# Attention and a two-layer MLP on one core: side work dealt out over the attention rounds, and one load moved from SyncE's queue to ScalarE's

## The chip, the cores and the metric

The kernel runs on 1 core of one Trainium2 chip. The metric is the device time of one execution in microseconds; lower is better. The times of the kernel before are 578.52, 578.22 and 577.88 us, median 578.22 us.

## The reference

Causal attention over 4 batches and 12 heads (sequence 448, head dimension 64), then a two-layer MLP with a PReLU on the 1792 tokens of width 768. Everything is float32.

```python
scores = scale * np.matmul(q, k.transpose(0, 1, 3, 2))
scores = np.where(mask, -1000000000.0, scores)
scores = scores - np.max(scores, axis=-1, keepdims=True)
attn = np.exp(scores)
attn = attn / (np.sum(attn, axis=-1, keepdims=True) + 1e-09)
x = np.matmul(attn, v).transpose(0, 2, 1, 3).reshape(1792, 768)
h = x @ w_in                                  # 768 x 2048
g = np.maximum(h, 0.0) + alpha * np.minimum(h, 0.0)
return g @ w_out                              # 2048 x 768
```

## The kernel before

**Attention, in rounds.** The 12 heads of a batch are taken in pairs, so there are 24 pairs of heads, numbered 0 to 23 in the order of the program. The work of a pair is spread over five rounds and the rounds overlap: round n loads pair n (`LK`, `LQ`: k and q by DMA on SP, line 473), makes the scores of pair n-1 on TensorE (`S0`, `S1`, `S2`, lines 563 and 555), masks them and takes row maxima of pair n-2 on VectorE (`MX..`, line 576), their exponentials and row sums on ScalarE (`EX..`, line 591), reciprocals on VectorE (`RC`, lines 604 and 605) and the normalisation on GpSimd (`NO..p`, line 534); transposes pair n-3 on TensorE (`PT..`, line 642) and copies the result out of PSUM to `ptf` (`C..`, ScalarE line 530 or VectorE line 532); and for pair n-4 does the products with v (`AV`, line 661, then `AH`, line 669), sums the outputs into the operands of the first GEMM (`XF`, line 693), copies out the part that is kept (`XH`, ScalarE line 530) and takes its low part (`XL`, line 723). The string `ORDER` (line 41) is this order, written out by hand; the number behind a `+` is how many rounds the step lies behind the loads, and the letter a, d or p behind it is the engine. Rounds 2 and 3 have strings of their own (`ROUNDS`, line 44), and `attention()` (line 796) changes the string for some others. Each engine takes its instructions in this order.

**V.** The first 64 rows of each causal block of 128 go through a block diagonal of V: `vd` (line 487), four buffers that GpSimd clears once (line 495) and that `load_vd(p)` (line 497, step `LW`) fills for pair p by two DMAs of 64x4x64, one for each head. `AH` of pair p multiplies by it. In the kernel before, all `LW` are issued on SP: those of pairs 0 and 1 in round 3, where the string has `LW+3 LW+2`.

**The hardware queues' semaphores.** The DMAs issued by SP and by ScalarE share eight completion semaphores (`DMAHW0` to `DMAHW7`), which the build hands out in turn over both engines; each such DMA first waits, in its engine's stream, for the DMA that had the same semaphore before it.

**Operands of the first GEMM.** It is done by a seven-product scheme of the Strassen kind. Each float32 operand is split into a high part and a low part. The sums of four weight blocks (`S1` to `S4`, `a_sum`, line 354, VectorE line 356), of pieces of x (`T1` to `T4`), their high parts (`h`, `t_hi`, on GpSimd, lines 733 and 534) and low parts (`l`, `t_lo`, line 736, VectorE line 737), the high parts of weights (`pcast` on GpSimd, line 534; `cast` on ScalarE, line 530) and their low parts (`sub`, GpSimd line 390) are needed from round 26 on. They are set into the attention rounds as side work, by tables: `EARLY` (line 26) names for each round its side steps, and `GAP`, `FRONT`, `MID`, `REAR` the same for other places. `plan_early()` (line 824) puts them in place: up to round 23, `l` and `S:` of `EARLY` go to `EG`, which stands after `LW` and before `XF` and `RC`; from round 24 on to `ED`, behind the copies `C..` of the round; those of `GAP` always to `EG`.

**After the attention** a planner (class `Plan`) orders the rest: the first GEMM (line 408), the PReLU, and the second GEMM (line 1342). Its output is the same for both kernels.

Of the kernel before, what the change touches and what calls it, by code (L numbers as in the profile page):

```python
# [23 lines left out]
QP = 128  # L24
WARM = 8
EARLY = {
# [4 lines left out]
}  # L31
GAP = {}
FRONT = {10: "LD", 16: "LD"}
MID = {26: "u u u"}
REAR = {}
# [5 lines left out]
ORDER = """  # L41
# [2 lines left out]
ROUNDS = {2: """  # L44
LK+0 LQ+0 EX10+2 EX11+2 MX00+2 EX00+2 MX01+2 EX01+2 MX20+2 EX20+2 MX21+2 EX21+2 RA+2 NO10+2p NO11+2p NO00+2p NO01+2p MX30+2 S0+1 S1+1 PT1+2 PT0+2 MX10+1 MX11+1 EX30+2 RB+2 NO20+2p NO21+2d NO30+2p
""", 3: """
LK+0 LQ+0 EX10+2 EX11+2 MX00+2 EX00+2 MX01+2 EX01+2 MX20+2 S2+2 EX20+2 MX21+2 PT2+3 EX21+2 C00+3d C20+3a C21+3d C10+3d S0+1 S1+1 SF+1 LW+3 LW+2 MX30+2 EX30+2 RC+2 NO10+2p NO11+2p NO00+2p NO01+2p NO20+2p NO21+2p NO30+2p MX10+1 MX11+1
"""}


# [143 lines left out]
def kernel(  # L194
# [10 lines left out]
    nc = tc.nc  # L205
    B, NPAIR, D, _, S = qt.shape
# [4 lines left out]
    LQ = S - NQ * QP  # L211
# [249 lines left out]
    T, vs, p3, masks, qd, vd = {}, [], [], [], [], []  # L461

    def half(j):
        return slice(j * D, (j + 1) * D)
# [32 lines left out]
    def load_vd(p):  # L497

        b, hp = pairs[p]
        for j in range(2):  # L500
            x = v[b, hp, :LQ, j]
            stride = x.ap[0][0]
            x = bass.AP(tensor=x.tensor, offset=x.offset, ap=[list(x.ap[0]), [(QP - CP) * stride + 2 * D, NQ + 1], list(x.ap[-1])])
            nc.sync.dma_start(out=vd[p % 4][half(j), :, j], in_=x)

    def load_v(b):
        for hs, n in ((hs, n) for hs in ((slice(0, NK), slice(NK, NPAIR)) if b == 0 else (slice(0, NPAIR),)) for n in range(NQ)):
# [242 lines left out]
    def t_four():  # L750
# [4 lines left out]
        "LV": load_v_next, "RC": row_rec, "RA": lambda p: row_rec(p, slice(0, 4)),  # L755
        "RB": lambda p: row_rec(p, slice(4, 2 * NQ + 1)), "AV": av, "AH": av_halves,
        "PTH": transpose_halves, "LW": load_vd, "BB": lambda p: None, "XH": x_hi, "XF": x_sums, "XL": x_lo,
        "ST": lambda p: flush(stores), "XN": lambda p: None, "LT": lambda p: None,
    }
# [25 lines left out]
    def order_of(text):  # L785
        order = []
        for w in text.split():
            name, lag = w.split("+")
            if name in choice:
                eng = {"a": nc.scalar, "d": nc.vector, "p": nc.gpsimd}[lag[-1]]  # L790
                order.append((int(lag[:-1]), name, lambda p, fn=choice[name], eng=eng: fn(p, eng)))
            else:
                order.append((int(lag), name, steps[name]))
        return order

    def attention(hooks):
        order, first = order_of(ORDER), {n: order_of(x) for n, x in ROUNDS.items()}

        for n in (5, 6, 7, 11, 12, 13, 20, 21, 22, 23):
            text = ORDER.replace("C00+3a", "C00+3d") if n in (5, 6, 11, 20, 22) else ORDER  # L800
            if n in (6, 7, 12, 13, 21, 23):
                text = text.replace("C30+4a ", "").replace("MX20+2 ", "MX20+2 C30+4d ")
            first[n] = order_of(text)
        first[1], first[4] = order_of(ORDER.replace("LW+1 ", "")), order_of(ORDER.replace("C00+3a", "C00+3d").replace("LW+1", "LW+2 LW+1"))

        text = ORDER.replace("C10+3a ", "").replace("EH+4 ", "EH+4 C10+3a ").replace("PT2+3 ", "PT2+3 PTH+3 ")
        first[26] = order_of(text.replace("C21+3d ", "C21+3d C30+3d "))
        first[27] = order_of(ORDER.replace("PTH+4 ", "").replace("C30+4a ", ""))
        last = max(lag for lag, *_ in order)
        for n in range(len(pairs) + last):  # L810
            for lag, name, fn in first.get(n, order):
                if 0 <= n - lag < len(pairs):
                    fn(n - lag)
                    for hook in hooks.get((n - lag, name), ()):
                        hook()
# [8 lines left out]
    def plan_early():  # L824
        for table, to in ((EARLY, plan), (GAP, gap), (FRONT, front), (MID, mid), (REAR, behind_it)):
            for n, todo in table.items():
# [50 lines left out]
    def ready_bank():  # L877

        b = ring.popleft()
        nc.tensor.matmul(b[:, :S], wi[0, "A11"][:, 0, :P], x1h[:, 0, 0], start=True, stop=True, skip_group_check=True)  # L880
        return b
# [66 lines left out]
    with tc.manual_schedule():  # L948
# [15 lines left out]
        for t in masks:  # L964
# [5 lines left out]
            out=mk, in_=mk, pattern=[[-1, QP]], compare_op=ALU.is_ge, fill=NEG, base=0,  # L970
# [22 lines left out]
        after(last, "LT", scores_over)  # L993
        after(last, "AH", attention_over)
        attention(hooks)
        t13, t24 = (tf[:, 2 * i : 2 * i + 2].rearrange("p a k n -> p (a k n)") for i in range(2))
        rooms["t"], rooms["v"] = Slots([]), Slots([])
# [6 lines left out]
        v_, z, y, x = ring.popleft(), ready_bank(), ring.popleft(), ring.popleft()  # L1004
# [544 lines left out]
```

## Time and profile before

| what | value |
|---|---|
| median of the three runs | 578.22 us |
| profiled execution, its own time | 578.1 us |
| span of that execution in the profile | 576.3 us |
| TensorE matmul busy | 566.0 us (98%) |
| VectorE busy | 471.2 us (82%) |
| ScalarE busy | 385.2 us (67%) |
| GpSimd busy | 290.5 us (50%) |

The span is what the profile sees between the first and the last instruction; the device time of the same execution is 1.8 us longer. In the profile PE is TensorE's matmuls, PEld its weight loads, DVE VectorE, ACT ScalarE, POOL GpSimd and SP SyncE, which only issues DMAs; "ACTq", "SPq" and "POOLq" are the streams that issue them. L669 is line 669 of the kernel. In a timeline a row is a run of like instructions: start, time from the first start to the last end, engine, line, tiles (written <- read), size, count; in brackets the idle time of the engine just before, and what ended it.

### The profile page before, as it was taken

What the parts mean: (1) busy time and instruction counts of PE and PEld (TensorE: products, weight loads), DVE (VectorE), ACT (ScalarE), POOL (GpSimd) and SP (SyncE); (2) the same over time, 40 slices, a digit from 0 to 9 for tenths busy, and PEclk for the clock granted to TensorE, in tenths of its full rate; (3) what the DMA queues carried; (4) which work ended last, traced back from release to release, by engine and by line L of the source; (5) the groups of instructions that cost most, each with busy time, mean ns of one, the idle gap of its engine ahead of it and who ended that gap; (6) DMA issues with size and microseconds to landing.
All of it is one profiled execution on the core that took longest, in us unless ns stands there. A gap on an engine that the chain in (4) does not pass through costs nothing.

```text
span 576.3 us, 11537 instructions
## 1 busy us (share of the span) xinstructions
PE 566.0 (98%) x3921; PEld 502.0 (87%) x3921; DVE 471.2 (82%) x988; ACT 385.2 (67%) x905; POOL 290.5 (50%) x338
## 2 busy tenths in 40 slices
PE   7999999999999999999999999999989999999997
PEld 4677767777788999999999999999989999999997
DVE  5798899999769887678877687798997899797763
ACT  5899987989778565665657556696755666665431
POOL 7766678897732543444445431446145543357420
PEclk9999999999999999999999999999999999999999
DMA  7755845644246575747777656692353424412532
GB/s 177 205 131 147 218 124 153 179 116 125 82 148 209 201 250 208 259 176 231 260 226 233 199 201 221 200 341 99 101 156 110 117 66 130 129 46 83 184 110 109
DMA packets 94074, 95.92 MB, mean 166 GB/s; under 512 B 24096, under 2 KB 83136, under 8 KB 94016
## 3 DMA queue, kind: packets, MB, share of 16 engines
q1 hardware_dynamic: 93168, 93.65, 53.2%
q0 software_dynamic: 528, 1.08, 0.6%
q8 instruction: 31, 0.51, 0.4%
q10 hardware_dynamic: 320, 0.46, 0.3%
q14 instruction: 27, 0.22, 0.1%
HBM read 66.85 MB, written 28.31 MB: 165 GB/s over the span
## 4 chain that ended last, share of the span: by engine, by line
PE 79%; DVE 14%; ACT 4%; issue 2%; DMA 1%; POOL 1%; ACTq 0%; DVEq 0%; POOLq 0%
PE bank L408 36%; PE bank L1342 32%; DVE bank L576 4%; PE bank L563 3%; ACT p L591 3%; PE bank L642 3%; PE bank L661 2%; DVE x1l L737 1%; DVE ptf L532 1%; PE bank L669 1%; PE bank L633 1%; DVE tf L693 1%; DMA kr<-in_k_dram 1%; DVE sm L604 1%; DVE nm L576 1%
## 5 line engine op out<-in xcount | busy, mean ns | idle before, releaser
L534 POOL TENSOR_SCALAR p<-p,rs 128x320 f32<-128x320 f32 (+3 forms) x165 | 83.4, 525 | 38.4 <-DVE rs L605 22.9
L1342 PE MATMUL bank<-x1h,x1l 128*128 128x384 f32 x540 | 98.7, 335 | 1.0 <-DVE x1h L1279 0.9
L1342 PEld LDWEIGHTS bank<-x1h,x1l 128*128 128x128 f32 x540 | 94.3, 188 | 1.6 <-DVE x1h L1279 1.2
L591 ACT ACTIVATE p<-bank,nm 128x192 f32<-128x192 f32 (+3 forms) x168 | 81.6, 510 | 16.4 <-DVE nm L576 15.9
L576 DVE CUSTOM_DVE_ANT_0 bank<-bank,mask 128x192 f32<-128x192 f32 (+3 forms) x168 | 70.4, 487 | 6.2 <-PE bank L563 5.8
L432 ACT ACTIVATE tf<-bank 128x448 f32<-128x448 f32 x64 | 34.5, 544 | 40.9 <-PE bank L408 30.9
L563 PE MATMUL bank<-kr,qr 64*128 64x320 f32 (+2 forms) x288 | 52.7, 451 | 1.0 <-DMA kr<-in_k_dram 0.5
L436 DVE SCALAR_TENSOR_TENSOR tf<-tf,om,bank 128x448 f32<-128x448 f32 x64 | 41.8, 676 | 6.8 <-ACT tf L432 6.5
L408 PE MATMUL bank<-x1h,wir 128*128 128x448 f32 x192 | 44.7, 368 | 0.0
L1342 PE MATMUL bank<-x1h,gset 128*128 128x384 f32 x216 | 40.4, 338 | 0.9 <-DVE acc L1355 0.9
L563 PEld LDWEIGHTS bank<-kr,qr 64*128 64x128 f32 x288 | 29.1, 186 | 11.7 <-ACT p L591 3.2
L1342 PEld LDWEIGHTS bank<-x1h,gset 128*128 128x128 f32 x216 | 37.9, 188 | 1.2 <-ACT acc L1476 1.2
L642 PE MATMUL bank<-ident,p 128*128 128x128 f32 x288 | 37.5, 278 | 1.5 <-POOL p L534 1.4
L408 PEld LDWEIGHTS bank<-x1h,wir 128*128 128x128 f32 x192 | 35.9, 188 | 3.4
L331 POOL TENSOR_TENSOR dec<-dec,tf 128x768 int32<-128x768 int32 x11 | 22.1, 2005 | 30.0 <-ACT tf L432 15.8
L591 ACT ACTIVATION_READ_ACCUMULATOR p<-bank,nm 128x1 f32 x168 | 36.9, 219 | 0.0
L530 ACT ACTIVATE ptf<-bank 128x384 f32<-128x384 f32 (+2 forms) x81 | 35.1, 499 | 2.6 <-PE bank L642 1.6
L661 PE MATMUL bank<-ptf,v 128*64 128x384 f32 (+2 forms) x288 | 36.1, 380 | 0.0
L1320 POOL TENSOR_TENSOR x1l<-acc,x1l 128x512 fp32r<-128x512 f32 x12 | 16.4, 1364 | 39.1 <-ACT x1l L1316 30.1
L422 DVE TENSOR_TENSOR bank<-bank,tf 128x448 f32<-128x448 f32 x30 | 18.9, 631 | 20.8 <-PE bank L408 18.2
L642 PEld LDWEIGHTS bank<-ident,p 128*128 128x128 f32 x288 | 31.1, 140 | 4.5 <-POOL p L534 2.9
L408 PE MATMUL bank<-x1h,wie 128*128 128x448 f32 x144 | 33.4, 367 | 0.0
(196 smaller groups left out, 1399.9 us busy)
## 6 DMA issues: line engine op xcount, KB each, us to landing
gd<-tf SPq DMA_DIRECT2D x64, 224.0 KB, 2.0
tf<-gd SPq DMA_DIRECT2D x28, 256.0 KB, 4.5
acc<-gd SPq DMA_DIRECT2D x28, 256.0 KB, 4.4
dec<-in_moe_w_in_dram SPq DMA_DIRECT2D x9, 768.0 KB, 5.2
tf<-in_moe_w_in_dram SPq DMA_DIRECT2D x7, 768.0 KB, 4.6
dec<-in_moe_w_out_dram SPq DMA_DIRECT2D x7, 768.0 KB, 4.8
tf<-in_moe_w_out_dram SPq DMA_DIRECT2D x7, 768.0 KB, 4.3
dec<-wd SPq DMA_DIRECT2D x13, 384.0 KB, 4.7
```

What stands on the lines that cost most here:

```text
L331: nc.gpsimd.tensor_tensor(out=y, in0=y, in1=low, op=ALU.add)
L408: nc.tensor.matmul(ps, w[:, u, k * P : (k + 1) * P], x[:, k], start=(st in ("P1", "P5") and i == 0), stop=(i == len(mms) - 1), skip_group_ ...
L432: nc.scalar.activation(t, bank_of(g, b, role), AF.Relu, scale=-1.0)
L436: stt(out=t, in0=t, scalar=om[:, f : f + 1], in1=bank_of(g, b, role), op0=ALU.mult, op1=ALU.add)
L530: eng.activation(out, x, AF.Copy, scale=side)
L534: eng.tensor_scalar(out=out, in0=x, scalar1=side, scalar2=1.0, op0=ALU.mult, op1=ALU.mult)
L563: nc.tensor.matmul(ps[:, o : o + lim], T["q", p][half(j), i * QP : (i + 1) * QP], T["k", p][half(j), :lim], start=(o == 0), stop=(n > 0 or ...
L576: nc.vector.tensor_tensor_reduce(out=t, in0=t, in1=mask_of(i), scale=-SCALE, scalar=MOST_F32, op0=ALU.add, op1=ALU.min, accum_out=nm,)
L591: nc.scalar.activation(T["p", p, i][:, j, : t.shape[1]], t, AF.Exp, scale=-1.0, bias=T.pop(("nm", p, i, j)), accum_out=T["sm", p][:, z : z ...
L642: nc.tensor.transpose(ps[:, j - js[0], c], t[:, j, c * QP : (c + 1) * QP], T["ident"])
L661: nc.tensor.matmul(out[half(j), c * QP + LQ :], vs[b % 2][:, hp, c, j], x[:, : (NQ - c) * QP], start=(c == 0), stop=False, skip_group_chec ...
L1342: nc.tensor.matmul(ps, x, w, start=(st in ("P1", "P5")[: 1 if Q else 2] and i == 0), stop=(i == len(mms) - 1), skip_group_check=True,)
```

## The change

It has three parts.

1. **`vd` of pair 0 goes through ScalarE's queue.** `load_vd` issues on `nc.scalar` for pair 0 and on `nc.sync` for the others. The step moves from round 3 (`LW+3` is gone from its string) to round 1 (`LQ+0 LW+1`), where the work of ScalarE is the opening of the program.
2. **The side work is dealt out again.** S2 goes from round 17 to 18, S3 from 18 to 24, S4 from 21 to 25. The low parts of x's sums, two in each of rounds 20, 23 and 24 and none in 21, 25 and 26 before, are one in each of rounds 18 to 26. One `h` goes from round 13 to round 23, so that there is one in each of rounds 11, 12 and 14 to 23. The counts are the same: four sums, twelve low parts, twelve high parts.
3. **One PSUM copy changes engine.** In round 11 the copy `C30` (line 530 on ScalarE) is done on VectorE (line 532), after the first maximum of 448 columns.

```diff
-    4: "LD", 5: "A:0", ... 11: "A:1 h", 12: "l I:1 C:1 h", 13: "D:1 h",
-    14: "G:1:0 +:1:0 h 4", 15: "G:1:1 +:1:1 4 h", 16: "l l 4 h", 17: "S:S1 S:S2 h pcast:A11", 18: "S:S3 l h sub:A11 pcast:S1",
-    19: "l sub:S1 h pcast:S2", 20: "l l sub:S2 h A:2", 21: "S:S4 h C:2", 22: "l h I:2", 23: "l l", 24: "l l",
-    25: "cast:A12 cast:S3 sub:A12 sub:S3", 26: "cast:S4 cast:A22 sub:S4 sub:A22 LD",
+    4: "LD", 5: "A:0", ... 11: "A:1 h", 12: "l I:1 C:1 h", 13: "D:1",
+    14: "G:1:0 +:1:0 h 4", 15: "G:1:1 +:1:1 4 h", 16: "l l 4 h", 17: "S:S1 h pcast:A11", 18: "S:S2 l h sub:A11 pcast:S1",
+    19: "l sub:S1 h pcast:S2", 20: "l sub:S2 h A:2", 21: "l h C:2", 22: "l h I:2", 23: "l h", 24: "S:S3 l",
+    25: "S:S4 cast:A12 cast:S3 sub:A12 sub:S3", 26: "cast:S4 cast:A22 sub:S4 sub:A22 LD",
-GAP = {}
+GAP = {25: "l", 26: "l"}
...
# ROUNDS[3]
-... S0+1 S1+1 SF+1 LW+3 LW+2 MX30+2 ...
+... S0+1 S1+1 SF+1 LW+2 MX30+2 ...
...
# load_vd
-            nc.sync.dma_start(out=vd[p % 4][half(j), :, j], in_=x)
+            (nc.sync if p else nc.scalar).dma_start(out=vd[p % 4][half(j), :, j], in_=x)
...
# attention()
-            if n in (6, 7, 12, 13, 21, 23):
+            if n in (6, 7, 11, 12, 13, 21, 23):
                 text = text.replace("C30+4a ", "").replace("MX20+2 ", "MX20+2 C30+4d ")
...
-        first[1], ... = order_of(ORDER.replace("LW+1 ", "")), ...
+        first[1], ... = order_of(ORDER.replace("LW+1 ", "").replace("LQ+0", "LQ+0 LW+1")), ...
```

Three places show the order of instructions.

ScalarE's stream at the start of the program, before: `mask` is the causal mask, `p` the exponentials of pair 0; in square brackets the semaphores that an instruction waits for.

```order
L973 ACT_TABLE_LOAD
L973 ACTIVATE mask_147<-tf 128x128 [waits Pool_49]
L976 ACTIVATE mask_148<-tf 64x64 x2
L591 ACTIVATE p_1_206,sm_207<-bank_62,nm_1_0_194 128x320 [waits DVE_49]
L591 ACTIVATE p_1_206,sm_207<-bank_63,nm_1_1_196 128x320 [waits DVE_49]
```

The same place in the changed kernel:

```order
L973 ACT_TABLE_LOAD
L973 ACTIVATE mask_147<-tf 128x128 [waits Pool_49]
L976 ACTIVATE mask_148<-tf 64x64 x2
L504 DMA vd_171<-in_v_dram 64x4x64 [waits DMAHW5_49,Pool_49]
L504 DMA vd_171<-in_v_dram 64x4x64 [waits DMAHW7_49]
L591 ACTIVATE p_1_208,sm_209<-bank_62,nm_1_0_196 128x320 [waits DVE_49]
L591 ACTIVATE p_1_208,sm_209<-bank_63,nm_1_1_198 128x320 [waits DVE_49]
```

The two DMAs now stand ahead of every exponential. Each waits for the DMA that had its semaphore before: `DMAHW5` is that of SP's first load of v below, `DMAHW7` that of SP's first half of k of pair 3.

SP's stream at the same time, in the changed kernel; before, the two rows of `vd_171` stood between `qd_102` and `vd_173`, with waits for `DMAHW5` and `DMAHW6`.

```order
L512 DMA v_167<-in_v_dram 80x3x128 [waits DMAHW5_49]
L512 DMA v_167<-in_v_dram 48x3x128 [waits DMAHW6_49]
L473 DMA kr_257<-in_k_dram 64x448 [waits DMAHW7_49,PE_49]
L473 DMA kr_257<-in_k_dram 64x448 [waits DMAHW0_49]
L473 DMA qr_260<-in_q_dram 64x384 [waits DMAHW1_49,DMASW0_49]
L473 DMA qr_260<-in_q_dram 64x384 [waits DMAHW2_49]
L477 DMA qd_102<-in_q_dram 64x3x64 [waits DMAHW3_49,DVE_49]
L477 DMA qd_102<-in_q_dram 64x3x64 [waits DMAHW4_49]
L504 DMA vd_173<-in_v_dram 64x4x64 [waits DMAHW6_49,Pool_49]
L504 DMA vd_173<-in_v_dram 64x4x64 [waits DMAHW0_49]
```

The order of SP's other DMAs is as before, and so are the semaphores of all that stand ahead of `vd_173`.

VectorE's stream in round 25, before, from the last maximum of the round to the start of round 26's side work: `x1l` is a low part, `tf` a sum of x, `sm` and `rs` the row sums and their reciprocals, `dec` a piece of weights.

```order
L576 ISA nm_3_0_2428 128x1
L693 TENSOR_TENSOR tf<-bank_65,tf 128x448
L604 TENSOR_TENSOR sm_2402<-sm_2402,least 128x7
L605 RECIPROCAL rs_2448<-sm_2402 128x7
L612 TENSOR_SCALAR p_1_2401<-p_1_2401,rs_2448 128x320 x2
L532 COPY ptf_2470<-bank_62 128x3x128
L319 TENSOR_SCALAR dec<-dec 128x768
L325 SCALAR_TENSOR_TENSOR dec<-dec 128x768
L693 TENSOR_TENSOR tf<-bank_63,tf 128x448
```

The same in the changed kernel:

```order
L576 ISA nm_3_0_2425 128x1
L737 TENSOR_TENSOR x1l<-tf,x1h 128x448
L693 TENSOR_TENSOR tf<-bank_65,tf 128x448
L604 TENSOR_TENSOR sm_2399<-sm_2399,least 128x7
L605 RECIPROCAL rs_2446<-sm_2399 128x7
L612 TENSOR_SCALAR p_1_2398<-p_1_2398,rs_2446 128x320 x2
L532 COPY ptf_2468<-bank_62 128x3x128
L356 TENSOR_TENSOR dec<-dec 128x384
L319 TENSOR_SCALAR dec<-dec 128x768
L325 SCALAR_TENSOR_TENSOR dec<-dec 128x768
L737 TENSOR_TENSOR x1l<-tf,x1h 128x448
L693 TENSOR_TENSOR tf<-bank_63,tf 128x448
```

A low part (line 737) has come in ahead of the sums of rounds 25 and 26, and S4 (line 356) ahead of the work on the third piece of weights. In rounds 20 and 23 the row of line 737 was there twice before and is there once now, between the last maximum and the sum of line 693.

## Rows read from the trace of the kernel before

**Rows 1.** The page: busy time and share of the span, by engine.

```profile
PE 566.0 (98%) x3921; PEld 502.0 (87%) x3921; DVE 471.2 (82%) x988; ACT 385.2 (67%) x905; POOL 290.5 (50%) x338
```

**Rows 2.** The chain that ended last, its late pieces: start us, us, what.

```profile
169.10 195.50 PE bank L408 x954
...
424.92 147.94 PE bank L1342 x846
```

**Rows 3.** The same chain at the start of the program.

```profile
7.25 1.14 ACT p L591 x4
...
18.42 0.69 PE bank L669 x16
```

**Rows 4.** Timeline of ACT, 0 to 9.6 us.

```profile
0.75 2.49 ACTq L473 DMA_DIRECT2D kr<-in_k_dram  x4
...
4.78 0.51 ACT L976 ACTIVATE mask<-tf 64x64 bf16<-64x64 f32 x2
7.25 0.53 ACT L591 ACTIVATE p<-bank,nm 128x320 f32<-128x320 f32 x1 [1.96 <-DVE nm L576]
```

**Rows 5.** Timeline of SP's stream, 0 to 16 us.

```profile
7.39 1.10 SPq L512 DMA_DIRECT2D v<-in_v_dram  x2
8.61 1.11 SPq L473 DMA_DIRECT2D kr<-in_k_dram  x2
...
12.48 2.61 SPq L504 DMA_DIRECT2D vd<-in_v_dram  x4
```

**Rows 6.** DMAs issued at 7.4, 8.6, 12.5 us: count, KB, us to landing.

```profile
v<-in_v_dram SPq DMA_DIRECT2D x1, 120.0 KB, 4.6
...
kr<-in_k_dram SPq DMA_DIRECT2D x1, 112.0 KB, 4.1
...
vd<-in_v_dram SPq DMA_DIRECT2D x1, 64.0 KB, 2.5
```

**Rows 7.** Waits of SP's stream, 0 to 8 us: total us, times, longest.

```profile
SPq L473 <- DMA kr<-in_k_dram: 0.7, 1, 0.7
```

**Rows 8.** Timeline of DVE, 6 to 19 us.

```profile
7.90 0.37 DVE L576 CUSTOM_DVE_ANT_0 bank<-bank,mask 128x192 f32<-128x192 f32 x1 [0.24 <-ACT p L591]
```

**Rows 9.** Timeline of PE, 0 to 20 us.

```profile
1.20 3.33 PE L458 MATMUL bank<-tf 128*128 128x512 bf16 x8 [1.20 <-DVE tf L952]
...
11.03 1.25 PE L642 MATMUL bank<-ident,p 128*128 128x128 f32 x5 [1.09 <-POOL p L534]
```

**Rows 10.** The page: granted clock of PE in 40 slices, 9 is 0.9 or more.

```profile
PEclk9999999999999999999999999999999999999999
```

**Rows 11.** Timeline of PE, `AH` of rounds 20 to 23.

```profile
117.32 0.66 PE L669 MATMUL bank<-ptf,vd 128*64 128x64 f32 x16
...
124.20 0.69 PE L669 MATMUL bank<-ptf,vd 128*64 128x64 f32 x16 [0.26 <-DVE ptf L532]
...
130.56 0.64 PE L669 MATMUL bank<-ptf,vd 128*64 128x64 f32 x16
...
136.33 0.64 PE L669 MATMUL bank<-ptf,vd 128*64 128x64 f32 x16
```

**Rows 12.** Timeline of DVE in rounds 20 and 21.

```profile
118.02 1.20 DVE L737 TENSOR_TENSOR x1l<-tf,x1h 128x448 fp32r<-128x448 f32 x2
...
119.68 1.63 DVE L604 TENSOR_TENSOR sm<-sm,least 128x7 f32<-128x7 f32 x1
...
125.41 1.11 DVE L356 TENSOR_TENSOR dec<-dec 128x384 f32<-128x384 f32 x1
```

**Rows 13.** Timeline of POOL in round 20.

```profile
119.29 1.00 POOL L390 TENSOR_TENSOR wie<-dec,wie 128x384 fp32r<-128x384 f32 x1
```

**Rows 14.** Timeline of PE's weight loads in round 23.

```profile
139.95 0.29 PEld L563 LDWEIGHTS bank<-kr,qr 64*128 64x128 f32 x2 [0.44 <-ACT low_B L530]
```

**Rows 15.** Timeline of DVE in rounds 25 and 26.

```profile
151.19 0.17 DVE L604 TENSOR_TENSOR sm<-sm,least 128x7 f32<-128x7 f32 x1 [0.95 <-ACT p L591]
...
157.20 0.62 DVE L693 TENSOR_TENSOR tf<-bank,tf 128x448 f32<-128x448 f32 x1 [2.02 <-PE bank L669]
```

More of the change, by code (lines that the diff above doesn't have):

```diff
@@ L46 @@
 """, 3: """
-LK+0 LQ+0 EX10+2 EX11+2 MX00+2 EX00+2 MX01+2 EX01+2 MX20+2 S2+2 EX20+2 MX21+2 PT2+3 EX21+2 C00+3d C20+3a C21+3d C10+3d S0+1 S1+1 SF+1 LW+3 LW+2 MX30+2 EX30+2 RC+2 NO10+2p NO11+2p NO00+2p NO01+2p NO20+2p NO21+2p NO30+2p MX10+1 MX11+1
+LK+0 LQ+0 EX10+2 EX11+2 MX00+2 EX00+2 MX01+2 EX01+2 MX20+2 S2+2 EX20+2 MX21+2 PT2+3 EX21+2 C00+3d C20+3a C21+3d C10+3d S0+1 S1+1 SF+1 LW+2 MX30+2 EX30+2 RC+2 NO10+2p NO11+2p NO00+2p NO01+2p NO20+2p NO21+2p NO30+2p MX10+1 MX11+1
 """}
@@ L800, in attention @@
             text = ORDER.replace("C00+3a", "C00+3d") if n in (5, 6, 11, 20, 22) else ORDER
-            if n in (6, 7, 12, 13, 21, 23):
+            if n in (6, 7, 11, 12, 13, 21, 23):
                 text = text.replace("C30+4a ", "").replace("MX20+2 ", "MX20+2 C30+4d ")
             first[n] = order_of(text)
-        first[1], first[4] = order_of(ORDER.replace("LW+1 ", "")), order_of(ORDER.replace("C00+3a", "C00+3d").replace("LW+1", "LW+2 LW+1"))
+        first[1], first[4] = order_of(ORDER.replace("LW+1 ", "").replace("LQ+0", "LQ+0 LW+1")), order_of(ORDER.replace("C00+3a", "C00+3d").replace("LW+1", "LW+2 LW+1"))
         text = ORDER.replace("C10+3a ", "").replace("EH+4 ", "EH+4 C10+3a ").replace("PT2+3 ", "PT2+3 PTH+3 ")
```

2 rows, old and new, of the table EARLY are left out of this document.

## The prediction

> **What bounds the kernel now.** I read the page's busy times first: TensorE's matmuls fill 98% of the span, VectorE 82%, ScalarE 67% [rows 1]. The chain of waits then says where that share is a bound and where it is not. From 169.10 us on it is TensorE's own work almost without a break [rows 2], so whatever is won or lost before that instant passes through to the end. In the first 18 us it is another chain: the exponentials of pair 0 at 7.25, and from there ScalarE, VectorE, GpSimd and the transposes by turns until the first `AH` at 18.42 [rows 3]. No DMA stands in that chain between 7.25 and 18.42, so if the first exponential comes later, so does the first `AH`. Between the two ends the pipeline of rounds runs; its beat is the distance of two `AH`. The shortest of rounds 20 to 23 is 5.77 us (130.56 to 136.33), that is TensorE's own work in a round; the others are 6.88 and 6.36 [rows 11], and what they have over 5.77 is what side work can cost or give back.
>
> The sum is made against the profiled execution, 578.1 us. The median of the runs is 578.22, 0.1 above, so the result is compared with either.
>
> **Part 1, `vd` of pair 0 on ScalarE's queue: +6.1.** Before, ScalarE ends the mask copies at 5.29 (4.78 + 0.51) and then idles 1.96 us until the first exponential at 7.25, which waits for VectorE's first maximum [rows 4]. Two issues fit into that idle time if they may go at once: four issues of ScalarE took 2.49, so 0.62 each, 1.25 together. But the order shows what each waits for. The first waits for `DMAHW5`, held by SP's first load of v, which is issued at 7.39 [rows 5] and lands 4.6 us later [rows 6], at 11.99. The second waits for `DMAHW7`, held by the first half of k of pair 3, issued at 8.61 [rows 5], landing 4.1 later [rows 6], at 12.71. SP's stream up to those two is unchanged, so I take the same instants. ScalarE's stream is in order, and every exponential stands behind these two DMAs. So: second issue from 12.71, plus 0.62, first exponential at 13.33 instead of 7.25: **6.1 us later**. That a DMA of one engine does wait in its stream for one of the other, the row of SP's waits shows: a load of k on SP stood 0.7 us until a load of k that ScalarE had issued was in [rows 7].
>
> Can the delay be caught up? VectorE's third maximum, at 7.90, waits for ScalarE's first exponential, since it uses the same PSUM bank [rows 8], so VectorE can do two maxima ahead and no more, and then runs through the same 11 us of work to the first `AH`. I count nothing back. Bounds of this term: 5.5 (12.71 - 7.25, if the issue costs the exponential nothing) and 6.6 (if the second landing takes the 4.6 of the first instead of 4.1).
>
> What SP gains by being rid of two issues (0.65 each of the 2.61 for four [rows 5]) is worth nothing: `vd` of pair 0 landed at about 15.0 (12.48 + 2.5 [rows 5, 6]) and is first needed at 18.42 [rows 3]. The Trainium skill (DMA: Bandwidth & Descriptors, section "Rules for kernel authors") says of spreading DMAs over several issuing engines that all run on the same 16 engines and only issue time on the sequencer is saved. By that rule alone this part would be worth 0, and the whole change 576.8; the semaphores above are what the rule leaves out, and they make it a loss.
>
> **TensorE after the longer wait: +0.8.** TensorE has done its scores by 9.94 and waits 1.09 us for the first transposes at 11.03 [rows 9]. Moved by 6.1 this becomes an idle time of 7.2 us. The granted clock reads 1.0 in all slices [rows 10], yet the opening row says that a rested array is slow: eight matmuls of 512 columns took 3.33 us, 0.416 each [rows 9], which is 1.23 columns per ns, the lower of the two levels (1.2 and 2.4 GHz). If the array comes back at the lower level at 17.1 (11.03 + 6.1) and needs as much work to get out of it as in the opening, half of 3.33 is lost, 1.7; nothing is lost where VectorE hides it. Bounds 0 and 1.7; I take the middle, 0.8, as VectorE and TensorE are both nearly full there. The Trainium skill (TensorE: Matmul & The Clock Gate, section "What's actually happening") has the array fall back to 1.2 GHz after an idle stretch; rows 9 agree for the start, and no row of this trace has an idle time in mid-program long enough to show it.
>
> **Part 2, the side work dealt out: -1.3.** Taken by rounds.
> - Round 20 loses one of two low parts, 0.6 us of VectorE (1.20 for two). Behind them stands line 604, which took 1.63 us from 119.68 [rows 12] where a free one takes 0.17 [rows 15]: it was held while GpSimd did two-operand work from 119.29 [rows 13]. 0.6 earlier it would end at 119.25, just ahead of GpSimd's. The round had 6.88 - 5.77 = 1.11 over TensorE's own work [rows 11]; that is the most to be had, nothing the least. VectorE is late there by its copy of `ptf` (0.26 [rows 11]). I take 0.7.
> - Round 23 loses one of two low parts likewise. The sum of line 693 and with it ScalarE's copy `low_B` come 0.6 earlier; TensorE's scores waited 0.44 for that copy [rows 14]. I take all of the 0.44.
> - Rounds 17 and 18: S2 moves one round on, S3 leaves; both were beside rounds that stand at TensorE's own work or close by. I take 0.2, bounds 0 and 0.6.
> - Round 21 has a low part (0.6) instead of S4 (1.11 [rows 12]), round 24 S3 instead of a low part: same count, 0, bounds -0.1 and +0.5.
> - Rounds 25 and 26 each get a low part, round 25 S4 too. VectorE idles 0.95 ahead of line 604 at 151.19 and 2.02 ahead of the sum at 157.20 [rows 15]. 0.6 goes into the first, 0.6 + 1.11 into the second. I count 0. If GpSimd's work holds them up as it did line 604, the second is overrun: up to +0.5.
> - The moved `h` I cost at nothing: GpSimd is 50% busy [rows 1] and `h` stands behind its normalisations. The copy of round 11 too: VectorE does it right after a maximum, and ScalarE has one copy less; if that cover fails, what is lost is of the size of one such side step, 0.6 at most.
>
> Sum: 0.7 + 0.44 + 0.2 = 1.3; bounds 0 and 2.5.
>
> **Total:** 578.1 + 6.1 + 0.8 - 1.3 = **583.7 us**.
>
> **Rivals.**
> 1. *The array stays at the upper level, or VectorE hides its slowness.* For it: the granted clock never fell below 1.0 [rows 10]. Against: the opening matmuls. 578.1 + 6.1 - 1.3 = 582.9. Chance 0.25.
> 2. *The dealing out gives nothing*, because GpSimd's two-operand work follows VectorE's about and holds it at another place. 578.1 + 6.9 = 585.0. Chance 0.06.
> 3. *Part of the hold is caught up*, by loads that have now 6 us more to land and by work done ahead in the first rounds. A third of the 6.1, without the clock: 578.1 + 4.1 - 1.3 = 580.9. Chance 0.05.
> 4. *ScalarE is not held* (the other side): the two DMAs go out in the idle 1.96 us at 5.29, or the exponentials don't queue behind them. Then the start is as before and only part 2 is left: 578.1 - 1.3 = 576.8. It decides if both landings come before 7.25 - 1.25 = 6.0 us, against 11.99 and 12.71 by the rows, so little speaks for it. Chance 0.06. With a third of the hold or less and the full 2.5 of part 2 the two would cancel: 0.03.
>
> **How the numbers follow.** The forecast, hold and slow array, has 0.55; the rivals 0.25, 0.06, 0.05, 0.06 and 0.03. A measurement of this kernel can tell about 0.2%, 1.2 us, from no change. Faster: rival 4, 0.06. Same: 0.03. Slower: the rest, 0.91. The range reaches down from rival 1 with part 2 near its best and the hold near 5.8 (578.1 + 5.8 - 2.5 = 581.4, I say 581.2) and up to the forecast with the array's whole 1.7 and the dealing out nearly void (578.1 + 6.3 + 1.7 - 0.5 = 585.6).
>
> **What would show it.** In ScalarE's timeline two issues of line 504, the second starting at about 12.7, and the first exponential at about 13.3; an idle time of 6 us or more on VectorE before its third maximum; the first `AH` at about 24.5 to 25.3; the first transposes after the gap slower than the 1.25 for five of before, if the clock falls. `AH` of rounds 20 and 21 less than 6.88 apart. From the start of the first GEMM on, all as before. A first exponential near 7.3 would refute part 1; a first `AH` below 24 would mean a catch-up that I excluded.

## The result, and the profile after

The changed kernel takes 583.77 us (median of 4 runs, 583.36 to 585.47) against 578.37 us of the kernel before beside it: a ratio of 1.0097, 95% interval 1.0074 to 1.0121, so 5.4 us slower. The forecast was 583.7. The profiled execution has 583.36 us and a span of 581.6. That the sum came out so close is partly luck: two of its terms were too small, and their errors have opposite signs.

The opening first. ScalarE's timeline of the changed kernel (start, time, stream, line):

```profile
5.38 0.50 ACT L976 ACTIVATE mask<-tf 64x64 bf16<-64x64 f32 x2
11.72 1.32 ACTq L504 DMA_DIRECT2D vd<-in_v_dram  x2
13.09 0.53 ACT L591 ACTIVATE p<-bank,nm 128x320 f32<-128x320 f32 x1 [7.20 <-DMA kr<-in_k_dram]
```

Against [rows 4], where 1.96 us of idle time ended with VectorE's first maximum, ScalarE now stands still for 7.20 us, and the view names a DMA, a load of k, as what released it. The first exponential comes at 13.09 instead of 7.25. The chain of waits says which transfer it really stood for, and the list of DMAs issued at 8.3 us (count, KB, us to landing) says when that load of k was in:

```profile
6.95 4.69 DMA v<-in_v_dram
...
11.72 0.65 ACTq L504
...
12.41 0.63 ACTq L504
```

```profile
kr<-in_k_dram SPq DMA_DIRECT2D x1, 112.0 KB, 3.8
```

SP's load of v is issued at 6.95 and lands at 11.64, then the first of the two DMAs of line 504 goes out, until 12.37; the 4.69 answers to the 4.6 of [rows 6]. The second goes out right behind it, at 12.41. Its holder, SP's first half of k of pair 3, was issued at 8.30 and took 3.8 us, so it was in at 12.1, while the first issue was still under way. Of the two holders that the order named, then, only the first held ScalarE; the second DMA cost no more than its own issue. SP's own timeline:

```profile
6.95 1.08 SPq L512 DMA_DIRECT2D v<-in_v_dram  x2
8.30 1.11 SPq L473 DMA_DIRECT2D kr<-in_k_dram  x2
...
12.17 1.25 SPq L504 DMA_DIRECT2D vd<-in_v_dram  x2
```

SP now issues two DMAs of `vd` instead of the four of [rows 5], and gains nothing by it. VectorE and TensorE stand still with ScalarE. VectorE's third maximum, at 7.90 in [rows 8]:

```profile
13.74 0.37 DVE L576 CUSTOM_DVE_ANT_0 bank<-bank,mask 128x192 f32<-128x192 f32 x1 [5.77 <-ACT p L591]
```

TensorE's timeline, where [rows 9] had an idle time of 1.09 us before the first transposes, and a stretch's busy times with the granted clock (the third number from the end):

```profile
14.76 1.86 PE L563 MATMUL bank<-kr,qr 64*128 64x448 f32 x2 [4.72 <-ACT p L591]
16.85 1.99 PE L642 MATMUL bank<-ident,p 128*128 128x128 f32 x6 [0.24 <-POOL p L534]
...
19.18 1.54 PE L642 MATMUL bank<-ident,p 128*128 128x128 f32 x6
20.66 3.57 PE L563 MATMUL bank<-kr,qr 64*128 64x320 f32 x12
...
26.10 0.63 PE L669 MATMUL bank<-ptf,vd 128*64 128x64 f32 x16
```

```profile
12.00:26.00 14.00, 10.91 (x62) 6.03 (x64) 10.53 (x45) 9.91 (x37) 8.13 (x16) 0.63 0.47 109
```

TensorE idled 4.72 us for the first exponentials, and the granted clock of the stretch is 0.63, where the kernel before has 1.00 in the same stretch: taken microsecond by microsecond it reads 0.50, the lower level, from 14.0 to 24.2, and 1.0 on both sides. The first `AH` is at 26.10, 7.68 later than in [rows 3]: 5.84 of it is the hold, the other 1.84 is lost between first exponential and first `AH`.

Where the 1.84 goes, the same rows of the kernel before show:

```profile
13.16 0.87 PE L642 MATMUL bank<-ident,p 128*128 128x128 f32 x6
13.96 2.16 PE L563 MATMUL bank<-kr,qr 64*128 64x320 f32 x12
```

Up to the first transposes nothing is lost: they come 3.76 us after the first exponential (16.85 - 13.09) and came 3.78 after it before (11.03 - 7.25, [rows 9] and [rows 3]). From there to the first `AH` it is 9.25 us instead of 7.39, and in between, at the lower level, six transposes and twelve scores take 5.11 instead of 3.03. The chain of the changed kernel is now TensorE's own work from 18.37 to the first `AH`, where the chain of the kernel before has ScalarE and VectorE by turns:

```profile
18.37 0.47 PE bank L642
...
20.73 3.50 PE bank L563 x12
...
24.97 1.30 PE bank L661 x12
```

So in this execution the lower level makes up the 1.84.

Then the rounds. `AH` of rounds 20 to 24:

```profile
123.92 0.63 PE L669 MATMUL bank<-ptf,vd 128*64 128x64 f32 x16
...
129.69 0.63 PE L669 MATMUL bank<-ptf,vd 128*64 128x64 f32 x16
...
136.44 0.64 PE L669 MATMUL bank<-ptf,vd 128*64 128x64 f32 x16
...
142.20 0.64 PE L669 MATMUL bank<-ptf,vd 128*64 128x64 f32 x16
...
148.18 0.64 PE L669 MATMUL bank<-ptf,vd 128*64 128x64 f32 x16
```

The distances are 5.77, 6.75, 5.76 and 5.98, against 6.88, 6.36, 5.77 in [rows 11] and 6.49 for the next. From the first `AH` to the last the changed kernel takes 147.25 us instead of 149.64, so 2.39 come back. At the start of the long stretch of GEMM, 5.29 are left (169.10 in [rows 2]), and they go through to the end, since the second GEMM starts 5.28 later:

```profile
174.39 195.51 PE bank L408 x954
...
430.20 147.94 PE bank L1342 x846
```

### The profile page after: what moved, and what is told of

It reads as the page before. It is cut to its first block, busy times and chain, and to the rows that moved or that the text cites. A ratio compares the mean times of both kernels' runs of the same rounds, so it can differ in the third digit from the quotient of the medians.

```text
span 581.6 us, 11540 instructions
## 1 busy us (share of the span) xinstructions
PE 568.9 (98%) x3921; PEld 503.6 (87%) x3921; DVE 471.4 (81%) x989; ACT 384.8 (66%) x904; POOL 290.1 (50%) x338
## 4 chain that ended last, share of the span: by engine, by line
PE 84%; DVE 9%; ACT 2%; DMA 2%; issue 1%; POOL 1%; ACTq 0%; SPq 0%; DVEq 0%; POOLq 0%
PE bank L408 36%; PE bank L1342 32%; PE bank L563 5%; PE bank L642 4%; PE bank L661 3%; DVE bank L576 2%; PE bank L633 2%; PE bank L669 1%; ACT p L591 1%; DVE tf L693 1%; POOL p L534 1%; DMA v<-in_v_dram 1%; DVE x1l L737 1%; DMA kr<-in_k_dram 1%; DVE ptf L532 1%
## 5 line engine op out<-in xcount | busy, mean ns | idle before, releaser
L576 DVE CUSTOM_DVE_ANT_0 bank<-bank,mask 128x192 f32<-128x192 f32 (+3 forms) x168 | 70.4, 483 | 12.1 <-PE bank L563 6.1
L563 PE MATMUL bank<-kr,qr 64*128 64x448 f32 (+2 forms) x288 | 55.5, 476 | 5.0 <-ACT p L591 4.7
L563 PEld LDWEIGHTS bank<-kr,qr 64*128 64x128 f32 x288 | 30.3, 198 | 16.4 <-ACT p L591 9.4
L530 ACT ACTIVATE ptf<-bank 128x256 f32<-128x256 f32 (+2 forms) x80 | 34.7, 501 | 2.9 <-PE bank L642 1.6
L661 PE MATMUL bank<-ptf,v 128*64 128x128 f32 (+2 forms) x288 | 35.3, 380 | 0.0
```

Of the source, the lines that this page charges most:

```text
L530: eng.activation(out, x, AF.Copy, scale=side)
L563: nc.tensor.matmul(ps[:, o : o + lim], T["q", p][half(j), i * QP : (i + 1) * QP], T["k", p][half(j), :lim], start=(o == 0), stop=(n > 0 or ...
L576: nc.vector.tensor_tensor_reduce(out=t, in0=t, in1=mask_of(i), scale=-SCALE, scalar=MOST_F32, op0=ALU.add, op1=ALU.min, accum_out=nm,)
L661: nc.tensor.matmul(out[half(j), c * QP + LQ :], vs[b % 2][:, hp, c, j], x[:, : (NQ - c) * QP], start=(c == 0), stop=False, skip_group_chec ...
```

## The experiments

Twelve kernels ran, in three groups, each group beside runs of the kernel before on the same chip. "Distance of AH" is always the time from one round's first matmul of line 669 to the next round's, in the profiled execution. The mean granted clock of an execution, 1 for the upper of TensorE's two levels and 0.5 for the lower, turned out to matter and is given where it does.

**Part 1 undone.** The diff puts `vd` of pair 0 back on SP in round 3 and keeps the rest of the change.

```diff
-... S0+1 S1+1 SF+1 LW+2 MX30+2 ...
+... S0+1 S1+1 SF+1 LW+3 LW+2 MX30+2 ...
-(nc.sync if p else nc.scalar).dma_start(out=vd[p % 4][half(j), :, j], in_=x)
+nc.sync.dma_start(out=vd[p % 4][half(j), :, j], in_=x)
-ORDER.replace("LW+1 ", "").replace("LQ+0", "LQ+0 LW+1")
+ORDER.replace("LW+1 ", "")
```

> The changed kernel with vd of pair 0 back on SP in round 3; the dealing out of the side work and the copy of round 11 stay. Theory (the hold of ScalarE's stream is the whole loss, the dealing out is a gain): first exponential at 7.2 to 7.4 us, first AH at 18.4, then 2.4 us won between the first and the last AH as in the changed kernel; 575.5 to 576.5 us. Rival (the dealing out brings nothing of its own, and what the changed kernel won between its AHs is only the late start caught up): 577.8 to 578.8.

577.45 us (575.88 to 578.55, 11 runs), ratio 0.9982 to the kernel before (0.9972 to 0.9992). The first exponential is at 7.25, as before. So the hold was the loss, 6.3 us of the medians, and the rest of the change is a gain. But the median missed its range by 1 us, and the profile shows a reason: the first `AH` came at 20.66, not 18.4, with a clock of 0.76 between 12 and 26 us.

```profile
12.00:26.00 14.00, 13.73 (x122) 9.28 (x124) 10.79 (x43) 9.24 (x35) 11.01 (x22) 0.76 0.68 195
```

```profile
11.03 1.25 PE L642 MATMUL bank<-ident,p 128*128 128x128 f32 x5 [1.09 <-POOL p L534]
12.55 0.47 PE L642 MATMUL bank<-ident,p 128*128 128x128 f32 x1 [0.27 <-POOL p L534]
```

Up to the second of these rows it is the program of the kernel before, with the same idle times of 1.09 and 0.27 us; a transpose that took 0.33 there takes 0.47 here. The clock reads 0.69 from 12 to 13 us, 0.50 from 13 to 19 and 0.90 from 19 to 20, so the array fell at 12.4 us and rose at 19.2. So the fall needs no long hold; the ordinary opening can bring it.

**Part 1 alone**, the same lines the other way round, on the kernel before.

> The kernel before with part 1 alone: vd of pair 0 on ScalarE in round 1, all else as before. Theory: first exponential at 13.1, first AH at 26.1 (7.7 later than before), and what part 2 won is missing, so 585.3 to 586.2 us. Rival (the late start is caught up in the middle whatever the tables say): 583.4 to 584.2, as the changed kernel.

585.43 us (585.02 to 585.96), ratio 1.0126 (1.0113 to 1.0139): 6.8 us slower. First exponential at 13.48, first `AH` at 25.72. Without the dealing out the loss is larger by 1.7 (though the two intervals touch), and from the first `AH` to the last the profile has 149.25 us against 149.64 before, so the middle does not catch it up. Part 1 is worth 6.8 and the rest of the change -1.7, of the medians; the forecast had 6.9 and -1.3.

**Keeping the array busy through the hold.** In the changed kernel, in `scores`:

```diff
         banks = [bank("s", p, n, j, uses=2 - n) for j in range(2)]
+        if p == 1 and n == 1:
+            for _ in range(26):
+                nc.tensor.matmul(banks[0], warm_sb[:, :P], warm_sb, start=True, stop=True)
```

> The changed kernel with 26 more bf16 matmuls of 512 columns, of zeros, into the PSUM bank of pair 1's third score, ahead of that score, so that TensorE works through most of the time in which ScalarE is held. Theory (of the 7.7 us at the first AH 5.8 are the hold and 1.8 the array at its lower level): first exponential still at 13.1, granted clock of the stretch 12 to 26 us near 1.0 instead of 0.63, first AH at 24.2 to 24.6, 581.4 to 582.2 us. Rival (the 1.8 us are waits of VectorE, GpSimd and ScalarE on one another): first AH at 26.0 or later, 583.2 or more.

582.77 us (581.87 to 585.1, 6 runs), ratio 1.0084 (1.0067 to 1.0101). The median moved 1.0 the way the theory has it and lies between the two ranges, and the intervals overlap with the changed kernel's. In the profiled execution the clock was 1.0 up to 19.1 us; after two more idle times of 1.09 and 0.27 it then read 0.50 from there to 22.5. The first exponential came at 13.51 there and the first `AH` at 25.45, 11.94 later, where it was 13.01 later in the changed kernel and 11.17 before: with a third of the changed kernel's time at the lower level, 0.77 is lost instead of 1.84. Three executions with a mean clock of 0.999 or 1.0 average 582.4, three below it 583.8. The price over many executions had to be found in another way (below).

**`vd` on ScalarE's queue, in round 3.** The changed kernel with `LW` of pair 0 where it was before, but on ScalarE.

```diff
-... S0+1 S1+1 SF+1 LW+2 MX30+2 ...
+... S0+1 S1+1 SF+1 LW+3 LW+2 MX30+2 ...
-ORDER.replace("LW+1 ", "").replace("LQ+0", "LQ+0 LW+1")
+ORDER.replace("LW+1 ", "")
```

> The changed kernel with vd of pair 0 still on ScalarE's queue, but in round 3, where SP issued it before; in ScalarE's stream the two DMAs then stand behind the exponentials of pair 0 and most of pair 1. Theory (the loss is the wait for semaphores whose earlier holders are still under way, and what stands behind it): first exponential at 7.2 to 7.4, ScalarE loses the two issues and a short wait, 1.0 to 1.5 us, at 15 us; 576.5 to 577.5 us. Rival (a load from ScalarE's queue costs this wherever it stands, or the load itself is slow): first AH later than 22, over 580.

578.64 us (577.85 to 579.51), ratio 1.0003 (0.9994 to 1.0013): 1.2 above the kernel with `vd` on SP, inside that theory's 1.0 to 1.5 for the loss, though the time itself was above the range since its base was. (None of its 11 executions had a mean clock over 0.997, two of the other kernel's 11 had; among those at 0.997 or less the difference is 1.0.) ScalarE's timeline:

```profile
14.49 2.64 ACTq L504 DMA_DIRECT2D vd<-in_v_dram  x2
17.18 0.31 ACT L591 ACTIVATE p<-bank,nm 128x64 f32<-128x64 f32 x1 [2.43 <-DMA vd<-in_v_dram]
```

Here the second DMA waits for `DMAHW6`, whose earlier holder is SP's second half of `vd` of pair 1; two issues that took 1.3 us elsewhere take 2.64, and the exponential behind them waits for that load, as the row names it. The hold has the length that its holder gives it.

**`vd` on GpSimd's queue**, in round 1 as in the change.

```diff
-(nc.sync if p else nc.scalar).dma_start(out=vd[p % 4][half(j), :, j], in_=x)
+(nc.sync if p else nc.gpsimd).dma_start(out=vd[p % 4][half(j), :, j], in_=x)
```

> The changed kernel with vd of pair 0 issued in round 1 as there, but on GpSimd's queue, whose DMAs have semaphores of their own; in GpSimd's stream they follow the first loads of v and wait for nothing still under way. Theory (what cost 6 us was the wait for SP's transfers in ScalarE's stream): first exponential at 7.2 to 7.4, no idle time of ScalarE over 2 us before it, time within 0.8 us of the 577.45 of the kernel with vd on SP. Rival (an early load of vd itself costs, because it delays the loads of q, k and v that are under way): over 579.

576.85 us (576.28 to 577.53), ratio 0.9972 (0.9961 to 0.9982); first exponential at 7.18. The early load of `vd` costs nothing by itself.

**Half of it on ScalarE, at the same place.** The other half goes out on SP, also in round 1. This is the run that separates the semaphore from the place in the stream.

```diff
-(nc.sync if p else nc.scalar).dma_start(out=vd[p % 4][half(j), :, j], in_=x)
+(nc.sync if p or j else nc.scalar).dma_start(out=vd[p % 4][half(j), :, j], in_=x)
```

> The changed kernel with the first half of vd of pair 0 on ScalarE's queue, at the same place in its stream ahead of every exponential, and the second half on SP in round 1. The semaphores fall out otherwise: ScalarE's DMA now waits for DMAHW3 with SP's first load of qd as its earlier holder, issued at 1.6 us, instead of two loads of 7 and 8 us. Theory (the loss is the wait for those two): ScalarE issues at 5.3 to 6, first exponential at 7.2 to 7.5, 576.0 to 577.8 us. Rival (a DMA ahead of the exponentials in ScalarE's stream holds them, whatever semaphore it has): first exponential at 9 or later, over 579.

576.96 us (575.66 to 577.7), ratio 0.9965 (0.9953 to 0.9977). ScalarE's timeline:

```profile
4.83 0.50 ACT L976 ACTIVATE mask<-tf 64x64 bf16<-64x64 f32 x2
6.16 0.67 ACTq L504 DMA_DIRECT2D vd<-in_v_dram  x1
6.88 0.53 ACT L591 ACTIVATE p<-bank,nm 128x320 f32<-128x320 f32 x1 [1.54 <-DVE nm L576]
```

The DMA stands just where the change put it, ahead of every exponential, waits 0.8 us for a load of `qd` that was issued at 1.6, and is out before VectorE's first maximum is ready; the exponential is at 6.88 and waits for VectorE, as before. So the issue from ScalarE is free there, and what cost 6 us was which semaphore the build had handed out.

**The array in the opening.** Six matmuls of zeros: five ahead of the first transposes, where TensorE idled 1.09 us, and one four transposes later; once on the kernel before, once on the change with `vd` on SP, once with `vd` on GpSimd's queue.

```diff
-            ps = bank("pt", p, i, js[0])[:, : len(js) * (i + 1) * QP]
+            ps = bank("pt", p, i, js[0])
+            for _ in range(5 if p == 0 and i == 1 else 1 if p == 0 and i == 0 else 0):
+                nc.tensor.matmul(ps, warm_sb[:, :P], warm_sb, start=True, stop=True)
+            ps = ps[:, : len(js) * (i + 1) * QP]
```

> The kernel before with the six bf16 matmuls of zeros ahead of the first transposes, nothing else. Theory (they keep the array at its upper level in the opening, which is worth what separates its executions of mean clock 1.0 from those of 0.994 to 0.997): mean clock 0.999 or 1.0 in most executions, 577.7 to 578.2 us. Rival (the win of the kernel with both is due to something else in the opening): mean clocks spread as before, 578.5.

> vd of pair 0 on SP, the dealing out kept, and six bf16 matmuls of zeros ahead of the first transposes (five into one PSUM bank, one into the next), where TensorE had idled 1.09 and 0.27 us. Theory (the opening's idle time is what lets the array fall to its lower level in some executions, also of the kernel before): granted clock 0.5 in no slice of 12 to 20 us, mean clock 0.998 or more in most executions, first AH at 18.4 to 18.8, 575.8 to 576.6 us. Rival (the level falls by chance, whatever TensorE does there): mean clocks spread as without them, 577.0 to 577.8.

> The changed kernel with vd of pair 0 on GpSimd's queue and the six bf16 matmuls of zeros ahead of the first transposes. Theory (the gain of the dealing out and that of the kept clock add up, and the queue of vd no longer matters): as the kernel with vd on SP and those matmuls, 575.4 to 576.4 us, mean clock 0.999 or 1.0. Rival (with vd on GpSimd's queue the clock was at its upper level anyway): as without them, 576.5 to 577.2.

| kernel | median us | ratio (95%) | mean clock of the executions |
|---|---|---|---|
| before + six matmuls | 578.01 (12 runs) | 0.9989 (0.9977 to 1.0000) | all 0.999 or 1.0 |
| change, `vd` on SP, + six | 575.99 (5 runs) | 0.9954 (0.9941 to 0.9968) | all 0.999 or 1.0 |
| change, `vd` on GpSimd, + six | 576.61 (6 runs) | 0.9959 (0.9943 to 0.9974) | all 0.999 or 1.0 |
| before, beside the three groups | 578.5 to 578.6 (72 runs) | | 33 at 0.999 or 1.0, 39 at 0.994 to 0.997 |

With the six matmuls not one of 23 executions had a mean clock under 0.999; without them more than half of those of the kernel before had. TensorE's timeline of "change, `vd` on SP, + six" shows what was filled: there is no idle time of 1.09 left, while the short one ahead of the sixth transpose is still there, 0.23 instead of 0.27.

```profile
10.08 1.25 PE L640 MATMUL bank<-tf 128*128 128x512 bf16 x5
...
12.74 0.33 PE L645 MATMUL bank<-ident,p 128*128 128x128 f32 x1 [0.23 <-POOL p L534]
```

The 33 average 578.08, the 39 average 578.97, so executions with the lower level take 0.9 us more, and the kernel before with the six matmuls takes what the 33 take; its own gain, 0.6 of the medians, is barely clear of noise. Where the level fell in the 39 can't be read, since one execution of each kernel has a trace. In all eight traces with a mean clock under 0.998 it fell between 11.9 and 21.8 us, and otherwise only in the last two microseconds. The stretch in which the change with `vd` on SP had 0.76, with the six matmuls:

```profile
12.00:26.00 14.00, 13.48 (x149) 9.05 (x148) 12.05 (x51) 10.71 (x39) 11.91 (x24) 1.00 0.75 193
```

The version with `vd` on SP, the dealing out and the six matmuls is faster than both kernels, 2.5 us under the one before. It is also 2.0 under the kernel before with the six matmuls, and as all executions of these two are at the upper level, that is the cleanest measure of parts 2 and 3. The version on GpSimd's queue cannot be told from it, but its median missed its range by 0.2 and lies in the one of its rival, the times without the matmuls. That rival's reason is refuted (six of the seven executions without them had 0.996 or 0.997), but a gain in time from the six matmuls isn't shown there: the intervals, 0.9961 to 0.9982 without and 0.9943 to 0.9974 with them, overlap. Its profiled execution lost 1.7 us in round 16 (a distance of 8.03), which the last section comes to.

**The dealing out in parts.** On the kernel before, the low parts alone, and the sums of weights alone:

```diff
# low parts only
-20: "l l sub:S2 h A:2", 21: "S:S4 h C:2", ... 23: "l l", 24: "l l",
+20: "l sub:S2 h A:2", 21: "S:S4 l h C:2", ... 23: "l", 24: "l",
-GAP = {}
+GAP = {25: "l", 26: "l"}
# sums only
-17: "S:S1 S:S2 h pcast:A11", 18: "S:S3 l h ...", ... 21: "S:S4 h C:2", ... 24: "l l", 25: "cast:A12 ..."
+17: "S:S1 h pcast:A11", 18: "S:S2 l h ...", ... 21: "h C:2", ... 24: "S:S3 l l", 25: "S:S4 cast:A12 ..."
```

> The kernel before with only the low parts dealt out (one fewer in rounds 20, 23 and 24, one more in 21, 25 and 26); the sums of weights, the h, the copy of round 11 and vd as before. Theory (rounds 20 and 23 are where the dealing out wins, by VectorE being free before GpSimd's two-operand work): AH of rounds 20 and 21 5.8 to 6.1 apart instead of 6.88, those of 23 and 24 6.0 instead of 6.49; 576.6 to 577.4 us at the same clock as before. Rival (the sums of weights win it): these distances stay at 6.9 and 6.5.

> The kernel before with only the sums of weights moved (S2 to round 18, S3 to 24, S4 to 25). Theory (they win what round 17 has over TensorE's own work, and the half of round 21): AH of rounds 16 and 17 6.2 to 6.5 apart instead of 6.85, 20 to 21 still 6.9, 21 to 22 5.8 to 6.4; 577.4 to 578.2 us. Rival (they win nothing or cost in rounds 24 and 25, where they come ahead of sums that TensorE waits for): round 17 as before, 24 to 26 longer, 578.6 or more.

577.61 us (576.46 to 578.99), ratio 0.9984 (0.9974 to 0.9994), and 578.50 us (577.14 to 580.08), ratio 1.0002 (0.9992 to 1.0013): both medians are above their ranges, by 0.2 and 0.3. Distances of AH, in us; a row is the distance up to that round:

| round | before | changed | lows only | sums only |
|---|---|---|---|---|
| 17 | 6.85 | 6.46 | 6.67 | 6.52 |
| 21 | 6.88 | 5.77 | 5.79 | 6.56 |
| 22 | 6.36 | 6.75 | 7.46 | 5.90 |
| 21 and 22 together | 13.24 | 12.52 | 13.25 | 12.46 |
| 24 | 6.49 | 5.98 | 5.95 | 6.66 |
| 25 | 6.06 | 5.99 | 5.77 | 6.78 |

The low parts alone win the 1.1 that I expected up to round 21 and give all of it back up to round 22; they win 0.5 in 24 and 0.3 in 25. The sums alone win the 0.8 of the two rounds, which is S4 gone from round 21, but lose 0.2 and 0.7 later, as the rival of that run had it. The 0.7 is S3 on top of two low parts, behind the copies of round 24; the next `AH` then waits 0.84 for ScalarE's copy:

```profile
144.89 0.76 DVE L356 TENSOR_TENSOR dec<-dec 128x384 f32<-128x384 f32 x1
145.58 1.40 DVE L737 TENSOR_TENSOR x1l<-tf,x1h 128x448 fp32r<-128x448 f32 x2
```

```profile
149.00 0.69 PE L669 MATMUL bank<-ptf,vd 128*64 128x64 f32 x16 [0.84 <-ACT ptf L530]
```

Only together do rounds 19 to 23 have one piece of such work each, and round 24 two where "sums only" has three. Each column is one profile, and single rounds move between profiles; the sum of rounds 21 and 22 is steadier. In the five profiles with S4 in round 21 it is 13.06 to 13.25, in the nine without 12.46 to 12.56 but for one of 12.97. VectorE's timeline of "lows only", and GpSimd's at the same time, show the give-back:

```profile
119.02 0.21 DVE L604 TENSOR_TENSOR sm<-sm,least 128x7 f32<-128x7 f32 x1 [0.42 <-ACT p L591]
...
123.33 0.55 DVE L356 TENSOR_TENSOR dec<-dec 128x384 f32<-128x384 f32 x1
123.80 2.15 DVE L737 TENSOR_TENSOR x1l<-tf,x1h 128x448 fp32r<-128x448 f32 x1
```

```profile
123.95 1.00 POOL L390 TENSOR_TENSOR wie<-dec,wie 128x384 fp32r<-128x384 f32 x1
124.93 0.56 POOL L534 TENSOR_SCALAR x1h<-tf 128x448 fp32r<-128x448 f32 x1
```

Line 604 is free now (0.21 instead of the 1.63 of [rows 12]), but the low part at 123.80, 0.62 when alone, is caught by GpSimd's work from 123.95 to 125.5 and takes 2.15. In "sums only", with two low parts in round 20 as before, line 604 is caught again:

```profile
119.37 1.64 DVE L604 TENSOR_TENSOR sm<-sm,least 128x7 f32<-128x7 f32 x1
```

```profile
118.98 1.00 POOL L390 TENSOR_TENSOR wie<-dec,wie 128x384 fp32r<-128x384 f32 x1
```

**The copy of round 11 alone.**

```diff
-            if n in (6, 7, 12, 13, 21, 23):
+            if n in (6, 7, 11, 12, 13, 21, 23):
```

> The kernel before with only the copy of round 11 on VectorE. Theory (the stall of that round is a late load of q, so the copy changes nothing): AH of rounds 11 and 12 6.4 to 6.7 apart, no other round changed by over 0.1, 577.9 to 579.0 us. Rival (the copy is what ScalarE was short of there): 5.8 to 6.2 apart.

578.25 us (576.75 to 580.49), ratio 0.9993 (0.9976 to 1.0011): no change. The distance up to round 12 was 6.52 (6.62 before), inside the theory's range. But other rounds did change, against the expectation: up to 17 it was 6.38 instead of 6.85, up to 24 6.82 instead of 6.49. Nothing of the program differs there, so a single round can move by some 0.5 us from one program to the next; I take it to be how VectorE's instructions fall on GpSimd's, which I did not follow up in these rounds. "Part 1 alone" had 6.69 up to round 17 as well.

## Why the prediction was right, and where it was not

- **Part 1, the hold: right in mechanism and size, but for the second wait.** Forecast: both DMAs held until 11.99 and 12.71, first exponential at 13.33. Measured: the first held until 11.64, the second by nothing but the first's issue, since its holder was in at 12.1, and the exponential at 13.09 (13.48 with part 1 alone). The number hardly shows it, because an issue of 0.65 stands where a wait of about that length was forecast. "SP's stream up to those two is unchanged, so I take the same instants" was right only within 0.4: SP issued the load of v at 6.95 instead of 7.39, and openings of profiled executions differ by as much. That SP gains nothing held too.
- **"I count nothing back": nearly.** VectorE waited 5.77 us for its third maximum and did two ahead, as forecast. The distance up to round 5 was 6.18 instead of 6.61, but in "part 1 alone" 6.58, so this is not the late start caught up. One reading was wrong without harm to the sum: between 7.25 and 18.42 the chain before holds ScalarE and VectorE alone, not GpSimd and the transposes.
- **TensorE after the longer wait: right that the array would fall, mis-sized.** The term was 0.8, from 1.7 halved. First exponential to first `AH` took 13.01 us in the changed kernel (26.10 - 13.09) and 11.17 before: 1.84, of which 0.43 came back up to round 5. Two steps of the term failed. The idle time was not one of 7.2 us but of 4.72 and 0.24, since the last two scores also wait for the first exponentials. And the array was not slow for half of 3.33 us with VectorE hiding a part: it was at the lower level from 14.0 to 24.2, the transposes and scores took 2.08 longer, and the chain ran through TensorE, so that VectorE hid next to nothing. That the unhalved 1.7 is close to 1.84 is luck. And the kernel before, which I took to be at the upper level throughout since its one profile was, has a lower mean clock in more than half of its executions, which take 0.9 us more. Against the median of before the term is smaller than against the profiled execution.
- **Part 2: right in sign, mis-sized, and the wrong steps were credited.** Forecast 1.3; the medians give 1.7 (part 1 alone against the changed kernel) and 1.2 (before against the changed kernel with `vd` on SP, whose executions had the lower clock more often), 2.0 with the six matmuls in both; between `AH` of rounds 5 and 27 it is 1.96. The step that failed is the 0.7 taken for round 20, with 0 for round 21. Freeing line 604 there moves the clash to the next round, and it is S4's move out of round 21 that wins the 0.72 of the two. Round 23's term was right: 0.44 forecast, 0.51 measured, 0.54 with the low parts alone. Rounds 17 and 18 took 0.44 less together where 0.2 was forecast, but they took 0.5 less with the copy of round 11 alone too, so that gain can't be put down to the sums. Rounds 25 and 26 took their new pieces free of charge, as forecast. The bounds "0 and 2.5" were not the sum of the terms' own, which reach 2.25 at best and a loss at worst.
- **Moved `h` and copy at nothing:** the copy held; the `h` alone was not tried.
- **The rivals.** That ScalarE is not held was refuted by its 7.20 us of idle time; that the dealing out gives nothing, by the runs without the hold; that a part of the hold is caught up, by part 1 alone, which won 0.4 us between its first and last `AH`. That the array stays at its upper level was refuted by the clock of 0.50, and that its slowness is hidden, by the rows of TensorE: the 1.84 lies in its transposes and scores. This is one profiled execution; the run that kept TensorE busy moved the median by 1.0 with overlapping intervals. That executions with the lower level take longer is shown on the kernel before.

## What to carry to other kernels

Here a DMA issued from ScalarE stopped all of ScalarE's stream until its completion semaphore was free, so before moving a DMA to an engine that also computes, look up which earlier DMA had the semaphore, when that lands, and what stands behind the wait; the idle time in front of the issue says nothing. A side step that is moved out of a round is worth what that round and the next lose together, not what the first one loses. And a start-up gap of one microsecond on TensorE can be filled with matmuls of zeros, after which no execution here showed the lower clock.

## What the runs showed of the hardware

- **The array falls to its lower level after short gaps.** In the opening TensorE idles 1.09 and 0.27 us, and 39 of 72 executions of the same program show a lower mean clock (0.994 to 0.997), 33 don't. In the profiled execution of the change with `vd` on SP the level fell at 12.4 us, after the first of those gaps and about at the second, and rose at 19.2. With the first gap filled by matmuls and the second left (0.23), none of 23 executions shows it. I had expected only the 7 us of the hold to bring it down.
- **VectorE and GpSimd shut each other out by whole instructions.** In the changed kernel the low part of round 22 takes 2.02 instead of 0.62 us, from just before GpSimd's two-operand instruction starts:

```profile
130.37 2.02 DVE L737 TENSOR_TENSOR x1l<-tf,x1h 128x448 fp32r<-128x448 f32 x1
```

```profile
130.39 1.00 POOL L390 TENSOR_TENSOR wie<-dec,wie 128x384 fp32r<-128x384 f32 x1
131.36 0.56 POOL L534 TENSOR_SCALAR x1h<-tf 128x448 fp32r<-128x448 f32 x1
```

  It ends at 132.39, 0.47 after GpSimd's second instruction: it waited for both of them and then ran. It goes the other way too. In the kernel before, a normalisation of 64 columns on GpSimd starts just behind the first of VectorE's two low parts of [rows 12] and ends at 119.32, 0.1 after the second; the like of it takes 0.32 in the changed kernel:

```profile
118.07 1.25 POOL L534 TENSOR_SCALAR p<-p,rs 128x64 f32<-128x64 f32 x1
```

```profile
130.12 0.32 POOL L534 TENSOR_SCALAR p<-p,rs 128x64 f32<-128x64 f32 x1
```

  With `vd` on GpSimd and the six matmuls the same happened to line 325 in round 16, 2.46 us, and that round was 8.03 long. The Trainium skill (SBUF — State Buffer, section "SBUF: two separate sides") states that a VectorE instruction with two SBUF inputs and a GpSimd instruction that reads SBUF exclude each other for the whole instruction; the rows agree. Which of the two comes first is decided by some tenths of a microsecond. In round 16 that is the 1.7 us between programs that are the same there; that the jumps of about 0.5 in other rounds have the same cause is likely, but not shown.
